# Output weights of a retention and bilinear kernel: six loads with casts on GpSimd, or six casting transfers from GpSimd's own DMA queue

## The chip, the core and the metric

The kernel runs on one core of one Trainium2 chip. The metric is device time in microseconds of one execution; before the change its median is 218.36 us over 3 runs (218.28 to 218.38).

## What is computed

A retention layer (linear attention with a decay for each head, 4 batches, 8 heads, 768 positions, head size 64) is followed by a bilinear feed-forward layer on 3072 tokens (model width 512, inner width 1536):

```python
for t in range(S):
    state = gamma * state + outer(k[:, :, t], v[:, :, t])      # per batch and head, 64 x 64
    y[:, :, t] = scale * q[:, :, t] @ state
x = y.transpose(0, 2, 1, 3).reshape(B * S, H * D)              # 3072 x 512
out = ((x @ w_a) * (x @ w_b)) @ w_out                          # w_a, w_b: 512 x 1536, w_out: 1536 x 512
```

All inputs and the output are f32. The change is about `w_out` alone.

## The kernel before

The 3072 positions are 24 chunks of 128. For each chunk GpSimd (or VectorE) multiplies k and q by a table of decays into a bf16 tile (`kqb`), a DMA transpose (later chunks) or TensorE (the first six) turns it into `kqT`, and TensorE forms masked scores (`at`, line 372), the running state (`st`, line 390) and the layer's output `y`. Finished chunks are gathered in groups of 4, 2, 2, 2, 2, 4 and 8 (`TILES`) for the feed-forward layer: `a` (line 568) and `g` (line 580) are the two products with `wa_bf` and `wb_bf`, ScalarE copies `a`, VectorE multiplies `g` with it into `ht`, and the product with `w_out` follows.

`w_out` lives on the chip as `wo_bf`, a bf16 tile of 128 partitions by 12 row blocks by 512 columns. It is used in three ways. For the first group, `ffn_out` (line 605) multiplies 4 pieces of 128 tokens with all 12 row blocks, 48 matmuls in the order of the blocks. For the later groups a Strassen-like scheme (`Group`, line 685) uses halves of `wo_bf` and sums of halves (`wsum`), which VectorE makes in `weight_sum` (line 618), right beside the first `ffn_out`. The first of these, `weight_sum(3)`, is two instructions on blocks 0 to 2 with 6 to 8, and 3 to 5 with 9 to 11.

Until the change `w_out` arrives in two steps. `load_o(j)`, called from the list `LOADS` through `issue_loads`, has SyncE's queue fetch two row blocks in f32 (512 KB, 2 KB to a packet) into a staging tile `wsto` of the pool `wstage` (6 buffers in turn, shared with the staging of the other weights and, later, with sums). `cast_o(j)` then has GpSimd cast it to bf16 into `wo_bf`. There are six of each (`NO`).

The order of the work on each engine is that of the program text: `seq` chains every instruction to the one before it on its engine. SyncE issues all loads of k, q, v and weights, the DMA transposes and the stores, one after the other, and a load that must wait for a buffer holds back all that is behind it. The entry of `LOADS` after the output weights, `s6`, loads chunks 6 and 7, and `t8` chunk 8; the DMA transposes of chunks 6 and 7 (line 333, in `casts_two`) come behind them. On GpSimd the six casts stand between the casts of v for the third pair of chunks (4 and 5) and the scaling of k and q for chunk 6 (line 292, from `casts_two(6)`).

Of the kernel before, what the change touches and what calls it, by code (L numbers as in the profile page):

```python
# [9 lines left out]
F32 = mybir.dt.float32  # L10
# [14 lines left out]
V_LATE = range(12, 20)  # L25
LACED = ("X3 X2 m1 m7 m2 a1 b1 a2 b2 m6 X1 a6 b6 a7 b7 F2 X4 m5 a5 b5 K20 G2 a3 b3 a4 b4 V18 "
         "m3 c1 d1 F3 H3 c2 d2 c6 d6 c7 d7 c5 d5 m4 c3 d3 V19 c4 d4 G3")
LOADS = "p0 p1 w0 w1 a1 b1 a2 k2 q2 b2 v2 o0 o1 o2 o3 o4 o5 s6 t8".split()


@with_exitstack
def kernel(
# [10 lines left out]
    nc = tc.nc  # L43
    P = 128
# [3 lines left out]
    DM = H * D  # L48
# [8 lines left out]
    FPO = NFT // NO  # L57
# [6 lines left out]
    wstage = ctx.enter_context(tc.tile_pool(name="wstage", bufs=6))  # L64
# [38 lines left out]
    def seq(bi):  # L103
        ins = bi.ins
        prev = last.get(ins.engine)
        if prev is not None:
            tc.add_manual_dep(ins, prev.name, nosync, reason="program order")
        last[ins.engine] = ins
        return bi
# [5 lines left out]
    raws, wst, whole = {}, {}, {}  # L115
# [19 lines left out]
    def load_two(nm, src, b, u, t):  # L135
        f = raw_tile([P, H, 2, D], F32, nm + "f", nm + "f")
        s = src[b, :, 2 * u * P : 2 * (u + 1) * P, :].rearrange("h (p two) d -> p h two d", two=2)
        seq(nc.sync.dma_start(out=f, in_=s))  # L138
        for par in range(2):
            raws[nm, t + par] = f[:, :, par, :]  # L140
# [5 lines left out]
    def load_wide(nm, n):  # L146
        src = {"a": moe_w_a, "b": moe_w_b}[nm]
        for i in range(2):
            st = wstage.tile([P, 2, 2 * WC], F32, tag="w", name="wst" + nm)
            s = src[2 * i * P : 2 * (i + 1) * P, 2 * n * WC : 2 * (n + 1) * WC]  # L150
            seq(nc.sync.dma_start(out=st, in_=s.rearrange("(c p) f -> p c f", p=P)))
            wst[nm, n, i] = st
# [7 lines left out]
            wst[nm, j] = st  # L160

    def load_o(j):
        st = wstage.tile([P, FPO, DM], F32, tag="w", name="wsto")
        s = moe_w_out[j * FPO * P : (j + 1) * FPO * P, :].rearrange("(c p) d -> p c d", p=P)
        seq(nc.sync.dma_start(out=st, in_=s))
        wst["o", j] = st

    pending = list(LOADS)

    def issue_loads(n):  # L170
        for _ in range(min(n, len(pending))):
            what = pending.pop(0)
            n = int(what[1:])
            if what[0] in "ab":
                load_wide(what[0], n)
            elif what[0] in "kqv":
                load_two(what[0], {"k": k, "q": q, "v": v}[what[0]], 0, n, 2 * n)
            else:
                {"p": load_pair, "s": load_slots, "t": load_slot, "w": load_w, "o": load_o}[what[0]](n)


    kqb = {}
    kqb = {}
    issue_loads(6)
    zero = osbp.tile([P, DM], F32, tag="osb", name="zero")
    seq(nc.vector.memset(zero, 0.0))
# [51 lines left out]
    wo_bf = wpool.tile([P, NFT, DM], BF16, name="wo_bf")  # L238
# [8 lines left out]
    def cast(engine, dst, src):  # L247
        if engine is nc.scalar:
            seq(nc.scalar.copy(dst, src))
        else:  # L250
            seq(engine.tensor_copy(dst, src))  # L251
# [8 lines left out]
    def cast_wide(nm, n):  # L260
        dst, c0 = {"a": wa_bf, "b": wb_bf}[nm], 2 * n * WC
        cast(nc.gpsimd, dst[:, :2, c0 : c0 + 2 * WC], wst[nm, n, 0])
        for i in range(2):
            c = slice(i * WC, (i + 1) * WC)
            cast(nc.gpsimd, dst[:, 2:, c0 + i * WC : c0 + (i + 1) * WC], wst[nm, n, 1][:, :, c])

    def cast_o(j):
        cast(nc.gpsimd, wo_bf[:, j * FPO : (j + 1) * FPO, :], wst["o", j])


    kb, qb, vb, kqT, aT = {}, {}, {}, {}, {}
# [808 lines left out]
    ffn_g(0, 0, 0, W2)  # L1080
    ffn_g(0, 1, 0, W2)
    issue_loads(100)
    cast_w(1, parts=2)
    ffn_a(0, 0, W2, 2 * W2)
# [30 lines left out]
    leave2(2, (A_, D_))  # L1115
    ffn_g(0, 11)
    for j in range(NO):
        cast_o(j)
    V_ = nc.vector

    def blocks(J, a, b):
# [147 lines left out]
```

## Time and profile before

| what | us |
| --- | --- |
| median of 3 runs | 218.36 |
| lowest and highest run | 218.28, 218.38 |
| span of the profiled execution | 216.6 |
| TensorE (PE) busy | 210.7 |
| GpSimd (POOL) busy | 154.2 |
| VectorE (DVE) busy | 147.5 |
| ScalarE (ACT) busy | 104.9 |
| one cast of a staging tile to `wo_bf`, of six | 1.04 |
| landing of one load of `wsto` after its issue, median | 8.7 |

The profile is one execution; its times count from the start of its span. The span leaves out what lies around the program on the device: 218.36 - 216.6 = 1.8 us beside the median of the runs. PE is TensorE's matmuls, PEld its weight loads, POOL is GpSimd, SPq the queue of DMAs that SyncE issues. A line of a timeline gives start, length, engine, line of the program, operation, what it writes and reads, how many, and in brackets how long the engine sat idle before and who ended that. "DMA to landing" counts from the issue to the arrival of the last byte.

### The profile page before, as it was taken

To read this page: it belongs to the slowest core of one execution; us is meant where nothing else is said; L and a number is where in the kernel's file an instruction comes from. 1 tells how busy PE (TensorE), PEld (TensorE's weight loads), DVE (VectorE), ACT (ScalarE), POOL (GpSimd) and SP (SyncE) were. 2 spreads that over 40 slices of the span, in tenths; PEclk is the share of its full clock that TensorE was granted. 3 is DMA by queue.
4 is the path that set the end of the run, shared out by engine and by line. 5 is a ranking of instruction groups with operands and counts; after the bars stand their busy time and mean duration, and the time that the engine had idled before them with its cause. 6 is when DMAs were issued, how large, how long until landed. Compare 5 with 4: busy or idle time off the path is not lost.

```text
span 216.6 us, 5713 instructions
## 1 busy us (share of the span) xinstructions
PE 210.7 (97%) x2252; PEld 146.1 (67%) x2252; DVE 147.5 (68%) x272; ACT 104.9 (48%) x235; POOL 154.2 (71%) x184
## 2 busy tenths in 40 slices
PE   7889999999999999999999999999999999999994
PEld 3557445587458888888888877457864444458883
DVE  3777346845984486356377978676577987688962
ACT  3256325343224444464576475657546656652331
POOL 5265876879878678969869979899986999530000
PEclk9999999999999999999999999999999999999999
DMA  5999999999999999999979999950013000000055
GB/s 162 290 320 365 387 311 360 384 268 232 221 264 227 228 231 222 158 192 269 197 169 245 222 209 234 236 127 3 5 69 125 2 0 3 2 0 0 27 194 170
DMA packets 85162, 39.68 MB, mean 183 GB/s; under 512 B 57488, under 2 KB 78864, under 8 KB 85136
## 3 DMA queue, kind: packets, MB, share of 16 engines
q1 hardware_dynamic: 84992, 39.26, 76.8%
q8 instruction: 17, 0.28, 0.5%
q14 instruction: 9, 0.07, 0.1%
q10 hardware_dynamic: 144, 0.07, 0.1%
HBM read 28.31 MB, written 6.29 MB: 160 GB/s over the span
## 4 chain that ended last, share of the span: by engine, by line
PE 91%; SPq 3%; DMA 3%; POOL 0%; issue 0%; DVE 0%
PE a L568 18%; PE g L580 18%; PE mA L685 12%; PE uA L859 10%; PE mB L685 6%; PE o L605 5%; PE uB L859 5%; SPq L138 3%; DMA wsta<-in_moe_w_a_dram 3%; PE mC L685 3%; PE at L372 2%; PE uC L859 2%; PE y L420 2%; PE st L390 2%; PE fa L949 2%; PE fb L949 1%
## 5 line engine op out<-in xcount | busy, mean ns | idle before, releaser
L582 DVE TENSOR_TENSOR ht<-g,asb 128x256 bf16<-128x256 f32 (+1 forms) x70 | 34.4, 493 | 31.6 <-PE g L580 28.0
L568 PE MATMUL a<-xt,wa_bf 128*128 128x256 bf16 (+1 forms) x280 | 48.6, 300 | 0.1
L580 PE MATMUL g<-xt,wb_bf 128*128 128x256 bf16 (+1 forms) x280 | 48.4, 300 | 0.0
L571 ACT CAST asb<-a 128x256 bf16<-128x256 f32 (+1 forms) x70 | 30.0, 429 | 33.3 <-PE a L568 31.1
L580 PEld LDWEIGHTS <-wb_bf 128*128 128x128 bf16 x280 | 27.0, 98 | 10.2 <-POOL wb_bf L251 0.2
L568 PEld LDWEIGHTS <-wa_bf 128*128 128x128 bf16 x280 | 26.5, 98 | 10.7 <-POOL wa_bf L251 0.4
L292 POOL TENSOR_TENSOR kqb<-kf,ktab 128x512 bf16<-128x512 f32 x22 | 23.6, 1078 | 7.4 <-DMA kf<-in_k_dram 4.9
L866 ACT COPY snap<-uA 128x512 f32<-128x512 f32 x36 | 20.0, 588 | 15.4 <-PE uA L859 13.9
L685 PEld LDWEIGHTS <-hs 128*128 128x128 bf16 x234 | 22.8, 98 | 3.6
L378 DVE TENSOR_TENSOR aT<-at,mask 128x512 bf16<-128x512 f32 x36 | 22.3, 682 | 0.3
L292 POOL TENSOR_TENSOR kqb<-qf,qtab 128x512 bf16<-128x512 f32 x18 | 19.6, 1088 | 2.7 <-DMA qf<-in_q_dram 2.7
L618 POOL TENSOR_TENSOR ht<-gsb,asb 128x512 bf16<-128x512 bf16 x13 | 15.2, 1175 | 7.5 <-DVE gsb L618 7.4
L692 ACT COPY snaps<-mA 128x256 f32<-128x256 f32 x30 | 11.0, 374 | 18.9 <-PE mA L685 18.9
L685 PEld LDWEIGHTS <-ht 128*128 128x128 bf16 x180 | 17.5, 98 | 3.3
L618 POOL TENSOR_TENSOR hs<-ht 128x384 bf16<-128x384 bf16 (+3 forms) x14 | 15.9, 1134 | 3.5 <-DVE ht L582 3.5
L618 POOL TENSOR_TENSOR hs<-ht,hs 128x384 bf16<-128x384 bf16 (+1 forms) x17 | 16.9, 997 | 1.5 <-DVE ht L582 1.4
L685 PE MATMUL mA<-wsum,hs 128*128 128x256 bf16 x120 | 15.2, 273 | 0.0
L618 DVE TENSOR_TENSOR osb<-mB,snaps 128x256 f32<-128x256 f32 x20 | 8.4, 421 | 8.3 <-ACT snaps L692 4.4
L251 POOL CAST vb<-vf 128x512 bf16<-128x512 f32 x12 | 7.5, 641 | 6.7 <-DMA vf<-in_v_dram 6.7
L605 PE MATMUL o<-wo_bf,ht 128*128 128x512 bf16 x48 | 10.7, 379 | 0.0
L618 DVE TENSOR_TENSOR asb<-uB,snap 128x512 bf16<-128x512 f32 x12 | 8.2, 685 | 3.1 <-ACT snap L866 2.0
L618 DVE TENSOR_TENSOR gsb<-uB,snap 128x512 bf16<-128x512 f32 x12 | 8.2, 686 | 2.9 <-ACT snap L866 2.1
(138 smaller groups left out, 374.7 us busy)
## 6 DMA issues: line engine op xcount, KB each, us to landing
qf<-in_q_dram SPq DMA_DIRECT2D x12, 512.0 KB, 6.1
out_dram<-osb SPq DMA_DIRECT2D x21, 256.0 KB, 4.1
kf<-in_k_dram SPq DMA_DIRECT2D x18, 256.0 KB, 5.1
vf<-in_v_dram SPq DMA_DIRECT2D x18, 256.0 KB, 5.3
wsta<-in_moe_w_a_dram SPq DMA_DIRECT2D x6, 512.0 KB, 7.7
wsto<-in_moe_w_out_dram SPq DMA_DIRECT2D x6, 512.0 KB, 8.7
wstb<-in_moe_w_b_dram SPq DMA_DIRECT2D x5, 512.0 KB, 8.3
kf<-in_k_dram SPq DMA_DIRECT2D x3, 512.0 KB, 7.1
```

The costliest lines, as they stand in the source:

```text
L292: seq(eng.tensor_tensor(dst, src, tab, op=ALU.mult))
L378: seq(nc.vector.tensor_tensor(aT[t][:, r], at[r], mask.to_broadcast([P, HP, P]), op=ALU.mult))
L568: seq(nc.tensor.matmul(a, wa_bf[:, kt, fs], xcols(J, kt, c0, c1), start=(kt == 0), stop=(kt == KT - 1)))
L571: seq(nc.scalar.copy(asb, a))
L580: seq(nc.tensor.matmul(g, wb_bf[:, kt, fs], xcols(J, kt, c0, c1), start=(kt == 0), stop=(kt == KT - 1)))
L582: seq(nc.vector.tensor_tensor(ht[J][:, ft, c0:c1], g, asbs.pop((J, ft, c0)), op=ALU.mult))
L605: seq(nc.tensor.matmul(o, ht[J][:, ft, i * P : (i + 1) * P], wo_bf[:, ft], start=(ft == 0), stop=(ft == NFT - 1), skip_group_check=True))
L618: seq(eng.tensor_tensor(dst, x, y, op=op))
L685: seq(nc.tensor.matmul(m, w, right[:, j], start=(first and j == 0), stop=(j == NP - 1), skip_group_check=True))
L692: seq(nc.scalar.copy(self.snaps[:, n], self.bank["A"]))
L859: seq(nc.tensor.matmul(m, w, right[:, k], start=(first and k == 0), stop=(k == 1), skip_group_check=True))
L866: seq(nc.scalar.copy(self.snaps[n], self.bank["A"]))
```

## The change

`load_o` no longer goes through SyncE and a staging tile. GpSimd issues the six transfers itself; each reads f32 from memory and writes bf16 into its part of `wo_bf`, so the cast happens in the transfer. The six casts are gone, and the six entries of `LOADS`. The transfers are issued where the casts stood in the program text.

```diff
-LOADS = "p0 p1 w0 w1 a1 b1 a2 k2 q2 b2 v2 o0 o1 o2 o3 o4 o5 s6 t8".split()
+LOADS = "p0 p1 w0 w1 a1 b1 a2 k2 q2 b2 v2 s6 t8".split()
...
     def load_o(j):
-        st = wstage.tile([P, FPO, DM], F32, tag="w", name="wsto")
         s = moe_w_out[j * FPO * P : (j + 1) * FPO * P, :].rearrange("(c p) d -> p c d", p=P)
-        seq(nc.sync.dma_start(out=st, in_=s))
-        wst["o", j] = st
+        seq(nc.gpsimd.dma_start(out=wo_bf[:, j * FPO : (j + 1) * FPO, :], in_=s))
...
-
-    def cast_o(j):
-        cast(nc.gpsimd, wo_bf[:, j * FPO : (j + 1) * FPO, :], wst["o", j])
...
     for j in range(NO):
-        cast_o(j)
+        load_o(j)
```

On GpSimd, between the casts of v for chunks 4 and 5 and the scaling of k and q for chunks 6 and 7, there stood before:

```order
L251 CAST vb<-vf 128x512 [waits DMAHW5_49]
L251 CAST vb<-vf 128x512
L251 CAST wo_bf<-wsto 128x1024 [waits DMAHW6_49]
L251 CAST wo_bf<-wsto 128x1024 [waits DMAHW7_49]
L251 CAST wo_bf<-wsto 128x1024 [waits DMAHW0_49]
L251 CAST wo_bf<-wsto 128x1024 [waits DMAHW1_49]
L251 CAST wo_bf<-wsto 128x1024 [waits DMAHW2_49]
L251 CAST wo_bf<-wsto 128x1024 [waits DMAHW3_49]
L292 TENSOR_TENSOR kqb<-kf,ktab_175 128x2x4x64 [waits DVE_49,DMAHW4_49,PE_49,Activation_49]
```

and with the change (line numbers of the changed file, 2 to 5 lower) there stands:

```order
L249 CAST vb<-vf 128x512 [waits DMAHW5_49]
L249 CAST vb<-vf 128x512
L164 DMA wo_bf<-in_moe_w_out_dram 128x2x512 x6
L287 TENSOR_TENSOR kqb<-kf,ktab_175 128x2x4x64 [waits DVE_49,DMAHW6_49,PE_49,Activation_49]
L287 TENSOR_TENSOR kqb<-qf,qtab 128x2x4x64 [waits DMAHW7_49]
```

Six casts that each waited for a load of SyncE became six DMA issues that wait for nothing of their own.

On SyncE, from the last load of the third pair of chunks on, there stood before:

```order
L138 DMA vf<-in_v_dram 128x8x128 [waits DMAHW5_49]
L165 DMA wsto<-in_moe_w_out_dram 128x2x512 [waits DMAHW6_49,Pool_49]
L165 DMA wsto<-in_moe_w_out_dram 128x2x512 [waits DMAHW7_49,Pool_49]
L165 DMA wsto<-in_moe_w_out_dram 128x2x512 [waits DMAHW0_49,Pool_49]
L165 DMA wsto<-in_moe_w_out_dram 128x2x512 [waits DMAHW1_49,Pool_49]
L165 DMA wsto<-in_moe_w_out_dram 128x2x512 [waits DMAHW3_49,DMAHW2_49,Pool_49]
L165 DMA wsto<-in_moe_w_out_dram 128x2x512 [waits DMAHW4_49,Pool_49]
L129 DMA kf<-in_k_dram 128x8x64
L138 DMA qf<-in_q_dram 128x8x128 [waits DMAHW5_49,DVE_49]
```

and with the change:

```order
L138 DMA vf<-in_v_dram 128x8x128 [waits DMAHW5_49]
L129 DMA kf<-in_k_dram 128x8x64 [waits DMAHW6_49]
L138 DMA qf<-in_q_dram 128x8x128 [waits DMAHW7_49,DVE_49]
L129 DMA kf<-in_k_dram 128x8x64 [waits DMAHW0_49]
L129 DMA vf<-in_v_dram 128x8x64 [waits DMAHW1_49]
```

The loads of chunks 6 to 8 moved up by six places.

On TensorE the order is the same; what the first product with `wo_bf` waits for is not. `o` is its result. Before:

```order
L605 LDWEIGHTS ht [waits DVE_49]
L605 MATMUL o<-wo_bf,ht 128x512 [waits Pool_49]
L605 LDWEIGHTS ht
L605 MATMUL o<-wo_bf,ht 128x512
L605 LDWEIGHTS ht
L605 MATMUL o<-wo_bf,ht 128x512 [waits Pool_49]
```

With the change:

```order
L600 LDWEIGHTS ht [waits DMASW0_49]
L600 MATMUL o<-wo_bf,ht 128x512 [waits DVE_49]
L600 LDWEIGHTS ht
L600 MATMUL o<-wo_bf,ht 128x512
L600 LDWEIGHTS ht
L600 MATMUL o<-wo_bf,ht 128x512 [waits DMASW1_49]
```

Each of the six waits for a cast by GpSimd is now a wait for one of GpSimd's transfers (DMASW0 to DMASW5), at every second matmul as before. VectorE's first `weight_sum` now waits for four of these transfers, and its second instruction for the other two.

More of the change, by code (lines that the diff above doesn't have):

```diff
@@ L178, in issue_loads @@
             else:
-                {"p": load_pair, "s": load_slots, "t": load_slot, "w": load_w, "o": load_o}[what[0]](n)
+                {"p": load_pair, "s": load_slots, "t": load_slot, "w": load_w}[what[0]](n)
     kqb = {}
```

## Prediction

> **What bounds the kernel now.** I read the page of the profile first (engine shares, the strip of 40 slices, the chain that ended last), then TensorE's waits, then a table by stretches around the place where the output weights are loaded and first used.
>
> ```profile
> span 216.6 us, 5713 instructions
> ...
> PE 210.7 (97%) x2252; PEld 146.1 (67%) x2252; DVE 147.5 (68%) x272; ACT 104.9 (48%) x235; POOL 154.2 (71%) x184
> ...
> DMA  5999999999999999999979999950013000000055
> ...
> PE 91%; SPq 3%; DMA 3%; POOL 0%; issue 0%; DVE 0%
> ```
>
> TensorE is busy 97% of the span and 91% of the chain of waits is TensorE. GpSimd (POOL) has 0% of the chain although it is 71% busy. The DMA engines are full for the first two thirds. So the question is whether TensorE ever waits for GpSimd or for a load.
>
> ```profile
> PE idle L552 <- DVE zero L186: 1.5, 1, 1.5
> PE tp L477 <- DVE kqb L292: 0.7, 3, 0.2
> PE idle L552 <- ACT kqT L249: 0.4, 1, 0.4
> ```
>
> That is the whole list of TensorE's waits: 2.6 us, none for a GpSimd cast and none for `wo_bf`. All three lines belong to the start of the program (warm-up matmuls and the first transposes); the rest of its idle time is the wait of the end for the last stores. The stretches around the change agree:
>
> ```profile
> 28.00:36.00 8.00, 8.00 (x51) 4.03 (x49) 4.85 (x7) 3.42 (x6) 5.44 (x8) 1.00 1.14 325
> 36.00:44.00 8.00, 8.00 (x123) 4.84 (x122) 6.34 (x11) 2.59 (x6) 6.34 (x8) 1.00 1.06 378
> 44.00:52.00 8.00, 8.00 (x75) 7.16 (x74) 3.82 (x9) 3.42 (x10) 6.13 (x7) 1.00 1.09 238
> 52.00:60.00 8.00, 8.00 (x43) 3.92 (x41) 7.50 (x10) 1.55 (x3) 6.81 (x8) 1.00 1.10 237
> ```
>
> The columns are start and end, length, then busy time and instructions of PE, PEld, DVE, ACT and POOL, the granted clock, the DMA share and GB/s. TensorE has 8.00 of 8.00 us in each stretch at a granted clock of 1.00: there is no idle time here that a faster GpSimd could return. The change can gain almost nothing; it can only lose, if TensorE begins to wait. The whole prediction is about deadlines.
>
> **The deadlines.** First use on TensorE, then on VectorE, then GpSimd's part as it stands:
>
> ```profile
> 52.66 7.93 PE L605 MATMUL o<-wo_bf,ht 128*128 128x512 bf16 x36
> 60.52 0.32 PE L390 MATMUL st<-vb,kqb 128*64 128x64 bf16 x8
> 60.76 0.64 PE L372 MATMUL at<-kqT 64*64 64x128 bf16 x32
> ```
>
> ```profile
> 53.27 1.86 DVE L618 TENSOR_TENSOR wsum<-wo_bf 128x768 bf16<-128x768 bf16 x2
> ```
>
> ```profile
> 37.70 1.18 POOL L251 CAST vb<-vf 128x512 bf16<-128x512 f32 x2 [0.59 <-DMA vf<-in_v_dram]
> 39.06 1.04 POOL L251 CAST wo_bf<-wsto 128x1024 bf16<-128x1024 f32 x1 [0.18 <-DMA wsto<-in_moe_w_out_dram]
> ...
> 45.87 1.04 POOL L251 CAST wo_bf<-wsto 128x1024 bf16<-128x1024 f32 x1 [0.38 <-DMA wsto<-in_moe_w_out_dram]
> 47.15 1.04 POOL L292 TENSOR_TENSOR kqb<-kf,ktab 128x512 bf16<-128x512 f32 x1 [0.23 <-PE a L568]
> ```
>
> The 36 matmuls of line 605 take 60.52 - 52.66 = 7.86 us, 0.22 us each. A sixth of `wo_bf` holds two of the twelve row blocks, so counting from 0, sixth j is wanted at 52.66 + 0.44 j: the first at 52.66 us, the last at 54.8 us. VectorE's first difference of weights (53.27) reads sixths 0, 1, 3 and 4, so it wants the fifth about a microsecond earlier than TensorE does; it can delay TensorE only later, through the work behind it. In before the last cast ends at 45.87 + 1.04 = 46.9 us: 5.7 us of slack before the first use.
>
> **Part by part: what leaves.** Six casts of 1.04 us (6.25 us) and the waits ahead of them (0.18 to 0.38 us each, 1.8 us in all) leave GpSimd: it went from 38.88 us (37.70 + 1.18) to 47.15 us with this block. Worth to TensorE: nothing, by the stretches above. Six issues leave SyncE's queue:
>
> ```profile
> 30.08 0.46 SPq L138 DMA_DIRECT2D vf<-in_v_dram  x1
> 30.63 6.88 SPq L165 DMA_DIRECT2D wsto<-in_moe_w_out_dram  x6
> 37.56 0.47 SPq L129 DMA_DIRECT2D kf<-in_k_dram  x1
> ...
> 51.83 4.17 SPq L333 DMA_TRANSPOSE kqT<-kqb  x2
> ```
>
> So the loads of k, q and v for chunks 6, 7 and 8, which began at 37.56, can begin at 30.63. That is earlier than needed and gains nothing either.
>
> **What comes.** Six DMA instructions on GpSimd at 38.88 us. They hold no wait, but they are behind everything GpSimd does until then: the transfers that were issued from 30.63 on now start over 8 us later. What one costs GpSimd no row shows. The nearest rows are the same transfer issued by SyncE and the cast that it replaces:
>
> ```profile
> L165 SPq DMA_DIRECT2D wsto<-in_moe_w_out_dram x6: 368/493/2011, 30.6 to 37.1; - x6
> ...
> DMA to landing us min/median/max: 8.1/8.7/9.6
> ```
>
> ```profile
> 38.12 3.90 SPq L138 DMA_DIRECT2D qf<-in_q_dram  x1
> ```
>
> The bounds are 0.37 us (SyncE's shortest for this transfer) and 3.9 us (its longest of any in this stretch, with the engines full). I take 1.04 us, the cast: GpSimd is then free at 38.88 + 6.24 = 45.1 us, 2 us earlier than before. Break-even against 47.15 is 1.38 us each. Behind the six stand the casts of chunks 6 and 7 and, on SyncE, the two transposes that wait for them:
>
> ```profile
> L333 SPq DMA_TRANSPOSE kqT<-kqb x2: 1250/2032/2813, 51.8 to 54.7; - x2
> ...
> DMA to landing us min/median/max: 3.2/4.1/5.0
> ```
>
> The second transpose lands at 54.7 + 3.2 = 57.9 us and TensorE reads it at 60.76, so GpSimd may be 2.9 us late: up to (47.15 + 2.9 - 38.88) / 6 = 1.86 us an issue before TensorE waits.
>
> The Trainium skill, "DMA: Bandwidth & Descriptors", section "Anatomy of one DMA", fits a GpSimd transfer at 2.0 us plus its bytes over 436 GB/s. By it one of these would take, as an estimate, 3.2 us, and six in a row with no overlap would end near 58 us instead of my 52; the same section says that most of the fixed part is waiting for the last byte, and the trace has six SyncE transfers overlapping (each 8.1 to 9.6 us to landing, all issued within 6.88 us), so I keep overlap. No row here shows GpSimd's own fixed part.
>
> **When the six land.** Now transfer rates, from three stretches in which one kind of load dominates (2 KB packets of the output weights, 256 B packets of k and v, 512 B packets at the start):
>
> ```profile
> 37.00:43.00 6.00, 6.00 (x80) 3.40 (x79) 5.44 (x9) 1.61 (x4) 4.42 (x6) 1.00 1.05 384
> 48.50:51.50 3.00, 3.00 (x30) 2.68 (x28) 1.59 (x4) 1.12 (x3) 2.37 (x3) 1.00 1.01 212
> 4.00:12.00 8.00, 7.32 (x86) 4.12 (x88) 5.99 (x11) 2.05 (x5) 2.65 (x4) 1.00 1.22 293
> ```
>
> A sixth (524 KB of f32) is 1.37 us of the engines at 384 GB/s, six are 8.2 us. Chunks 6 to 8 are six loads of 262 KB at 212 GB/s (1.24 us) and two of 524 KB at 293 GB/s (1.79 us): 11.0 us. The bare time to landing is read from the smallest transfer of the page:
>
> ```profile
> out_dram<-osb SPq DMA_DIRECT2D x1, 64.0 KB, 1.8
> ```
>
> which is 1.8 us. The v load ahead of them landed at 37.70, so its packets were through near 35.9 and the engines then work on chunks 6 to 8. When the first new transfer appears (38.88 + 1.04 = 39.9 us), 11.0 - 4.0 = 7.0 us of these are left, and the new 8.2 us compete with them; behind them come the transposes. How two queues share an engine no row shows. If they take turns packet by packet, a 2 KB packet (2048 B at 384/16 = 24 GB/s an engine, 85 ns) meets a 256 B one (19 ns) or a 512 B one (28 ns), so the new queue gets 75 to 82%. The six are through at 39.9 + 8.2/0.79 = 50.3 and land by 52.1 us. The sixths before it land about 1.7 us apart, so the first is there near 43.5: each has over 2 us to its deadline. If they share time equally, the last is through at 39.9 + 16.4 = 56.3 and lands at 58.1, or at 56.9 if SyncE's queue runs dry at 53.9. I take turns by packet, because a packet is the piece in which the engines' work stands in the trace.
>
> The Trainium skill, the same page, section "Queues, rings and completion order", has each engine go round its queues and drain a packet of typically 9 to 17 descriptors before it switches. With 16 rows of each kind that is 1.37 against 0.31 us, 82% for the new queue, and the sum would be as above; if the turns were of equal bytes it would be the equal-time rival below. No run so far shows two loaded queues.
>
> Casting inside the transfer is the other unknown. Its bounds are 0.68 us a sixth (by the bf16 bytes written, half as many) and 2.73 us (half the rate); I take 1.37 us, the f32 bytes read, which is the row's own.
>
> **Sum:** gain 0, loss 0 while every landing is ahead of its use. The profiled execution has a span of 216.6 us and the runs shown a median of 218.36 (218.28 to 218.38), 1.8 us around the span; what is around it I leave unchanged. Forecast 218.4 us.
>
> **Rivals.**
> *Equal shares* (16%). The queues share the engines by time, not by packet. For it: SyncE's queue is loaded without a break (DMA share 1.04 to 1.1 in every stretch above). Against it: the packet sizes differ eightfold. The last sixth lands 2.1 to 3.3 us after 54.8, TensorE waits at line 605 that long, and all behind it is late: about 221 us. It decides as soon as the new queue gets under 8.2/(54.8 - 1.8 - 39.9) = 63% of the engines.
> *Slow issue* (14%). GpSimd needs well over 1.86 us for one. At 2.5 us it is free at 53.9, 6.7 us late; the transposes land at 64.6 instead of 57.9 and TensorE waits 3.9 us at line 372 (what it may have waited before, for the last sixth, is part of it): about 222.3 us. At 3.9 us it would be some 12 us. For it: nothing in the trace shows GpSimd making a transfer. Against: SyncE makes one in 0.37 us when unhindered.
> *Slow cast* (13%). At half the rate the six take 16.4 us, at 79% of the engines 20.8 us, through at 60.7, landing at 62.5: TensorE waits 7.7 us, 226 us. It decides from about 1.3 times the plain rate.
> *A cost around the program* (5%): a queue that was not used before may add to what lies around the span, by an amount no row shows; I allow half a microsecond.
> *A small gain* (8%). GpSimd 2 us ahead and SyncE's loads 7 us ahead could remove delays of a tenth of a microsecond among the short matmuls; over 0.44 us would be needed to see it, and TensorE's own list holds no wait after the start to remove.
>
> **How the numbers follow.** No visible change has 44%, the likeliest single case, so the forecast is 218.4 us. A measurement of this kernel can tell about 0.2%, 0.44 us, from no change. Slower holds 16 + 14 + 13 + 5 = 48%, faster 8%. Slower altogether is a little likelier than no change, but it is spread over 219 to 226 us. The range runs from 217.8 (most of the small gain) to 222.6, which takes in equal shares and a slow issue up to 2.5 us, and leaves out the slow cast and the tails, under 2 in 10.
>
> **What would show it.** Right: in the changed profile TensorE's list has no line for `o` or `wo_bf`, the six issues take GpSimd about 1 us each from 38.9, the matmuls of line 600 (605 before) start at 52.7 and the first `at` at 60.8. Wrong: a TensorE wait on the DMA of `wo_bf` (equal shares, slow cast; the packets' own time tells which), or GpSimd's `kqb` later than 50 us with TensorE waiting for `kqT` (slow issue).

## The result, and the profile after

The median is **218.77 us** (9 runs, 218.64 to 219.47) against 218.28 us (9 runs, 218.19 to 218.38) of the kernel before beside it: ratio 1.0025, 95% interval 1.0015 to 1.0034. That is 0.49 us more: small, but every run of it lies above every run of before. The profiled execution's span went from 216.572 to 217.056 us, 0.484 us, so what lies around the span did not change.

The page of the changed kernel, engine shares, the strip of the DMA engines, the new queue and the chain that ended last:

```profile
span 217.1 us, 5711 instructions
...
PE 210.3 (97%) x2252; PEld 145.9 (67%) x2252; DVE 148.7 (68%) x272; ACT 104.8 (48%) x235; POOL 151.6 (70%) x184
...
DMA  6999999999999999999989999970022000000055
...
q0 software_dynamic: 1632, 1.57, 4.5%
...
PE 91%; SPq 3%; DMA 3%; POOL 0%; issue 0%; DVE 0%
```

Nothing moved at this scale, except that a queue `q0` appears: GpSimd's, with 1.57 MB (the bf16 bytes that it writes). TensorE's waits, the whole list again:

```profile
PE idle L547 <- DVE zero L184: 1.5, 1, 1.5
PE tp L472 <- DVE kqb L287: 1.1, 3, 0.5
PE idle L547 <- ACT kqT L247: 0.4, 1, 0.4
```

No line for `o` and none for `wo_bf`. The first uses on TensorE stand where they stood:

```profile
52.71 7.93 PE L600 MATMUL o<-wo_bf,ht 128*128 128x512 bf16 x36
60.57 0.32 PE L385 MATMUL st<-vb,kqb 128*64 128x64 bf16 x8
60.82 0.64 PE L367 MATMUL at<-kqT 64*64 64x128 bf16 x32
```

Each is 0.05 us later than before, as is the last matmul of the program (it starts at 213.32 instead of 213.27). GpSimd's timeline around the change, and the six transfers as a group:

```profile
38.88 4.50 POOL L164 DMA_DIRECT2D wo_bf<-in_moe_w_out_dram  x6
43.36 1.10 POOL L287 TENSOR_TENSOR kqb<-kf,ktab 128x512 bf16<-128x512 f32 x1
...
51.10 0.61 POOL L249 CAST vb<-vf 128x512 bf16<-128x512 f32 x1 [3.12 <-DMA vf<-in_v_dram]
53.61 1.16 POOL L287 TENSOR_TENSOR kqb<-kf,ktab 128x512 bf16<-128x512 f32 x1 [1.90 <-DMA kf<-in_k_dram]
```

```profile
L164 POOL DMA_DIRECT2D wo_bf<-in_moe_w_out_dram x6: 732/750/900, 38.9 to 42.6; - x6
...
DMA to landing us min/median/max: 5.4/8.4/11.1
```

Six issues take 4.50 us. The transfers land at 44.28, 45.80, 48.15, 50.30, 51.55 and 53.68 us (the first is 38.88 + 5.4, the last 42.6 + 11.1). TensorE wants the last at 52.71 + 5 x 0.44 = 54.9, so it comes 1.2 us ahead. GpSimd is 3.8 us ahead of before at 43.36, and then waits 3.12 and 1.90 us for loads of chunks that TensorE reads only after 60 us.

**Where the half microsecond is.** SyncE's work ends with a walk: it checks the semaphores of all DMA queues (and two of VectorE and ScalarE, numbers 100 and 107 in the trace), two to an instruction, and then the program ends. These are the rows of that walk on the program's last line, of before and of after (number, duration in ns, first and last start):

```profile
L1264 SPq EVENT_SEMAPHORE  x7: 17/28/28, 214.8 to 216.5; - x7
```

```profile
L1259 SPq EVENT_SEMAPHORE  x10: 17/28/28, 215.7 to 217.0; - x10
```

Three more checks: GpSimd's six transfers brought six semaphores, which six of SyncE's eight are paired with. But the number alone is not it. After the last store has landed (215.65 before, 215.70 after), what is still to be walked differs. Of after, the stretch from 215.75 to 216.19, and of before all from 215.66 to the end:

```profile
L1259 SPq EVENT_SEMAPHORE  x7: 27/28/28, 215.8 to 216.2; - x7
```

```profile
L1264 SPq EVENT_SEMAPHORE  x4: 17/22/28, 215.7 to 216.5; - x4
L1264 SPq DRAIN  x3: 7/7/13, 215.8 to 216.1; - x3
```

After: the store's own pair is checked at 215.72, and these seven follow, 0.44 us at about 0.065 us each. Before: the first of the four is the store's own pair (215.67), one more follows (215.73), and the last two belong to the drains behind the walk, which both kernels have. From the landing of the last store to the end it is 0.92 us before and 1.35 us after: 0.43 of the 0.484 us. The rest is the 0.05 us that the last store is later.

Not all of the 0.43 us is the walk. From the check of the store's own pair to the first drain behind the walk it is 0.13 us before and 0.51 after, 0.38 more, for six more pairs. From that drain to the end it is 0.78 and 0.83 us. GpSimd clears semaphores there, and SyncE's last check waits for it; the clear takes longer after than before:

```profile
L1264 POOLq EVENT_SEMAPHORE_RANGE_CLEAR  x1: 96/96/96, 216.2 to 216.2; - x1
```

```profile
L1259 POOLq EVENT_SEMAPHORE_RANGE_CLEAR  x1: 139/139/139, 216.6 to 216.6; - x1
```

The place in the walk is set by which of SyncE's eight semaphores the last store gets: they go round, one for each DMA that SyncE issues (and one for the single store that ScalarE issues). The last store in the order of the two kernels, before and after:

```
118 L754 DMA out_dram<-osb 128x128 [waits DMAHW6_49,DVE_49]
112 L749 DMA out_dram<-osb 128x128 [waits DMAHW0_49,DVE_49]
```

Six issues fewer on SyncE shift it by six of eight, from the seventh semaphore (number 109 in the trace) to the first (101). The walk goes 105 and 104, 106 and 103, 108 and 101, 109 and 100, 110 and 107 before the change; afterwards 101 with GpSimd's 116 is the first pair of eight. Before, the walk is nearly over when the last store lands; now it waits at its first pair and has seven to go.

### The profile page after: what moved, and what is told of

Its sections match the earlier page's. It is cut to its first block, busy times and chain, and to the rows that moved or that the text cites. A ratio compares the mean times of both kernels' runs of the same rounds, so it can differ in the third digit from the quotient of the medians.

```text
span 217.1 us, 5711 instructions
## 1 busy us (share of the span) xinstructions
PE 210.3 (97%) x2252; PEld 145.9 (67%) x2252; DVE 148.7 (68%) x272; ACT 104.8 (48%) x235; POOL 151.6 (70%) x184
## 3 DMA queue, kind: packets, MB, share of 16 engines
q0 software_dynamic: 1632, 1.57, 4.5%
## 4 chain that ended last, share of the span: by engine, by line
PE 91%; SPq 3%; DMA 3%; POOL 0%; issue 0%; DVE 0%
PE a L563 18%; PE g L575 18%; PE mA L680 12%; PE uA L854 10%; PE mB L680 6%; PE o L600 5%; PE uB L854 5%; SPq L138 3%; DMA wsta<-in_moe_w_a_dram 3%; PE mC L680 3%; PE at L367 2%; PE uC L854 2%; PE y L415 2%; PE st L385 2%; PE fa L944 2%; PE fb L944 1%
```

## The experiments

The expectations letter the theories. **A**: the half microsecond is the walk at the end, and depends on which semaphore the last store has. The rivals **B** and **C** have it come with GpSimd's transfers as such (its queue in use and its semaphores to be checked; work that they hold up in the body), whatever semaphore the last store has. **D** came up later, for a scatter between runs: the last transfer lands too near its use.

**after_lane**: the changed kernel with seven loads of q cut in two, so that the last store gets the semaphore that is checked last (110). All of GpSimd's transfers stay.

```diff
-        seq(nc.sync.dma_start(out=f, in_=s))
+        if nm == "q" and t in (10, 12, 14, 16, 18, 20, 22):
+            for r in range(2):
+                hs4 = slice(HP * r, HP * (r + 1))
+                seq(nc.sync.dma_start(out=f[:, hs4], in_=s[:, hs4]))
+        else:
+            seq(nc.sync.dma_start(out=f, in_=s))
```

> The changed kernel with seven loads of q (chunks 10 to 22) cut into two halves of four heads each, so that SyncE issues seven DMAs more and the last store of the program uses another of the eight DMA semaphores, the one that SyncE checks last at the end of the program. Theory A (the loss is made at the end: after the last store has landed SyncE still checks seven pairs of semaphores, 0.065 us a pair, because six more semaphores stand in the list and the last store's is now checked first): no pair is left to check after the landing, about 0.45 us less than the change, 218.3 us, level with before within 0.1 us. Theory B (GpSimd's queue costs its 0.4 us at the end or around the span however the checks are ordered): 218.75 us as the change. Theory C (TensorE loses it on the way): 218.75 us, with the last matmul later than in before.

Measured: 218.29 us (11 runs, 218.18 to 218.35) beside 218.26 of before, ratio 0.9999 (0.999 to 1.0008). The rows of the walk until the last store lands at 215.68 us, and from there:

```profile
L1264 SPq EVENT_SEMAPHORE  x7: 27/28/28, 214.2 to 215.5; - x7
```

```profile
L1264 SPq EVENT_SEMAPHORE  x3: 17/17/28, 215.7 to 216.5; - x3
L1264 SPq DRAIN  x3: 7/7/13, 215.8 to 216.1; - x3
```

Seven pairs are done before the landing, the eighth holds the last store (the first of the three checks), none is left. The end is 0.92 us behind the landing, as in before. The loss is gone with all six transfers in place: C falls, and B as the main part. A small part of B stays: GpSimd's clear takes 0.139 us here too, and from the first drain to the end it is 0.84 us, 0.06 over before. The kernel is level with before because it has one pair less to go behind the store.

**before_lane**: the other way round, the kernel before with five loads of q cut in two by the same lines (chunks 14 to 22), so that the last store gets number 105, in the first of the five pairs. No transfer of GpSimd's is in it.

```diff
+        if nm == "q" and t in (14, 16, 18, 20, 22):
```

> The kernel before with five loads of q (chunks 14 to 22) cut into two halves, nothing else: the last store now uses a semaphore that SyncE checks first of its five pairs instead of fourth. Theory A: four pairs to check after the landing instead of one, 3 x 0.065 = 0.2 us more than before, 218.5 us, with no GpSimd transfer in the program. Theories B and C: 218.3 us, as before.

Measured: 218.52 us (11 runs, 218.40 to 218.58), ratio 1.0011 (1.0002 to 1.0019): 0.26 us over before. Four pairs are left when the store lands at 215.74, and the end is 1.11 us behind it. Of the 0.26 us, 0.19 are the walk (1.11 - 0.92), the rest a last store that is 0.07 us later.

**before_spare**: the kernel before with six casting transfers at the end of GpSimd's program, into `wa_bf`, which nothing reads any more. Nothing is left out of the computation.

```diff
     big()
+    spare = wa_bf.rearrange("p a (b c) -> p (a b) c", c=DM)
+    for j in range(NO):
+        s = moe_w_out[j * FPO * P : (j + 1) * FPO * P, :].rearrange("(c p) d -> p c d", p=P)
+        seq(nc.gpsimd.dma_start(out=spare[:, j * FPO : (j + 1) * FPO, :], in_=s))
```

> The kernel before with six casting transfers of the output weights by GpSimd added at the end of its program, where GpSimd and the DMA engines have nothing else to do; they write over the weights of the first product, which nothing reads any more, and nothing waits for them but the end of the program. Theory A: SyncE checks eight pairs instead of five, but the last store keeps a semaphore near the end of the list, so nothing is left to add: 218.3 us, as before. Theory B: 0.4 us more, 218.7 us. It also measures the transfer by itself: with an empty set of engines I expect 0.75 us an issue as in the changed kernel, and 1.4 us between landings if casting costs the engines nothing beyond the f32 read, 2.7 if it halves their rate.

Measured: 218.32 us (11 runs, 218.19 to 219.06), ratio 1.0006 (0.9997 to 1.0014). Eight pairs are walked, but the last store still has 109, one pair is left, and the end is 0.96 us behind its landing: the 0.04 us over before are again the longer clear (0.138 us). Together:

| kernel | pairs in the walk | last store's semaphore | pairs left at its landing | landing to end, us | median, us |
| --- | --- | --- | --- | --- | --- |
| before | 5 | 109 | 1 | 0.92 | 218.28 |
| before_spare | 8 | 109 | 1 | 0.96 | 218.32 |
| after_lane | 8 | 110 | 0 | 0.92 | 218.29 |
| before_lane | 5 | 105 | 4 | 1.11 | 218.52 |
| after | 8 | 101 | 7 | 1.35 | 218.77 |

The time goes with the fourth column, not with the second; that GpSimd's transfers are there adds about 0.05 us.

The same run shows the six transfers nearly alone, at a time when SyncE's queue has little to do. The DMA queues from 193 to 206 us:

```profile
q0 software_dynamic: 1627, 1.57, 81.7%
q1 hardware_dynamic: 140, 0.13, 3.8%
```

They are packets of 1 KB (the bf16 written), about 104 ns each (81.7% of 16 engines' 13 us over 1627). From the first packet (195.5 us) to the last (206.5) it is 11.0 us, 1.8 us a transfer. In the changed kernel, against a loaded SyncE queue, it is 12.0 us (40.9 to 52.9): the load from SyncE slowed GpSimd's queue by about a tenth. The landings from the first to the last lie 53.68 - 44.28 = 9.4 us apart there; here 206.97 - 197.85 = 9.1 us.

**spare_plain**: is it the cast that makes a transfer take 1.8 us? The same six, f32 into f32, over `wa_bf` and `wb_bf` seen as f32 (nothing reads them any more; nothing is left out).

```diff
-    spare = wa_bf.rearrange("p a (b c) -> p (a b) c", c=DM)
     for j in range(NO):
+        spare = (wa_bf, wb_bf)[j // 3].rearrange("p a f -> p (a f)").bitcast(F32)
+        spare = spare[:, j % 3 * FPO * DM : (j % 3 + 1) * FPO * DM]
```

> The kernel before with six transfers by GpSimd of the same f32 data at the end of its program, as in before_spare, but without the cast: f32 into the place of the two other weights, which nothing reads any more. Nothing uses them. It separates the cast from the queue. In before_spare the six took 10.9 us alone (1.8 us each, 96 to 98 ns a packet). If casting is what costs, the six take about 8.2 to 8.6 us here, 1.4 us each, and 85 to 88 ns a packet as on SyncE's queue. If GpSimd's queue is what costs, they stay near 10.9 us. Time 218.3 us either way.

Measured: 218.22 us (one run). From 193 to 206 us:

```profile
q0 software_dynamic: 862, 3.14, 67.8%
q1 hardware_dynamic: 141, 0.13, 2.9%
```

Packets of 4 KB now and half as many, but 10.8 us for the six. The engines are 14 points less busy and the transfers hardly faster, so neither the cast nor full engines set this pace. It was seen only on GpSimd's queue: SyncE's six in the kernel before landed 1.36 us apart on average (39.01 to 45.82). What sets the pace was not found.

The Trainium skill, "DMA: Bandwidth & Descriptors", section "Bandwidth", gives 6.15 us and 341 GB/s for a transfer of 1 MB issued from GpSimd. The two do not go together if each byte is counted once: 1 MB in 6.15 us is some 170 GB/s, as an estimate from that row. Here 3.15 MB in six overlapping transfers take 10.8 us, 291 GB/s counted once, faster than the row's time would have it and slower than its rate; no run here has a single transfer of 1 MB, and the measurement decides for transfers of this size.

**late_issue**: how much slack is there, and what does a late transfer cost? The changed kernel with the six issues behind `casts_two(6)`, so 6.1 us later (44.97).

```diff
-    for j in range(NO):
-        load_o(j)
...
     casts_two(6)
+    for j in range(NO):
+        load_o(j)
```

> The changed kernel with the six transfers issued after GpSimd's casts of chunks 6 and 7 instead of before them, about 9 us later. In the changed kernel the last of the six landed at 53.7 us, about 1.1 us before TensorE wants it. By the deadlines of the prediction, the last should land at 58 to 63 us and TensorE wait 4 to 8 us at the first product with the output weights, all of it in the time: 222.5 to 227 us. If the first product could start late without loss (other work of TensorE in its place), the time would stay under 219.5.

Measured: 226.01 us (one run). TensorE's waits have a first line now, and TensorE's timeline shows each wait:

```profile
PE o L600 <- DMA wo_bf<-in_moe_w_out_dram: 4.3, 5, 1.2
```

```profile
52.69 0.59 PE L600 MATMUL o<-wo_bf,ht 128*128 128x512 bf16 x2
54.08 0.59 PE L600 MATMUL o<-wo_bf,ht 128*128 128x512 bf16 x2 [0.79 <-DMA wo_bf<-in_moe_w_out_dram]
55.73 0.59 PE L600 MATMUL o<-wo_bf,ht 128*128 128x512 bf16 x2 [1.06 <-DMA wo_bf<-in_moe_w_out_dram]
57.51 1.01 PE L600 MATMUL o<-wo_bf,ht 128*128 128x512 bf16 x2 [1.18 <-DMA wo_bf<-in_moe_w_out_dram]
```

The sixths land at 52.16, 54.04, 55.69, 57.47, 59.06 and 60.71 us. TensorE waits 4.3 us, yet the last matmul is 7.3 us later. The stretches say why (columns as before; the granted clock is third from the end):

```profile
52.00:60.00 8.00, 4.38 (x18) 1.70 (x17) 1.41 (x3) 0.37 (x1) 1.38 (x3) 0.80 1.22 196
60.00:64.00 4.00, 3.36 (x10) 1.21 (x9) 3.20 (x5) 0.59 (x1) 1.36 (x2) 0.55 1.12 225
```

A mean of 0.80 over 8 us and of 0.55 over 4 us is a clock of 0.5 for 1.6 / 0.5 + 1.8 / 0.5 = 6.8 us, from 56.75 us on, during the third wait: the same two matmuls take 1.01 instead of 0.59 us. The waits cost about 1.7 times their own length.

The Trainium skill, "TensorE: Matmul & The Clock Gate", Part 1, has the clock halved after an idle window of 3.4 us and restored after a busy one. The half rate and the length (two such windows) agree with this trace; the condition does not read the same here, since no wait was over 1.2 us and TensorE worked between them, 1.2 us of the 3.4 us ahead of the drop.

**early_issue**: is there a better place, ahead of everything in this block? The six issues ahead of the scaling of k for chunks 4 and 5, at 30.78 us.

```diff
     cast_wide("a", 2)
+    for j in range(NO):
+        load_o(j)
     casts2(2, {(K, 0): G_, (K, 1): G_}, ("b", 2))
...
-    for j in range(NO):
-        load_o(j)
     V_ = nc.vector
```

> The changed kernel with the six transfers issued 8 us earlier, ahead of GpSimd's scaling of k for chunks 4 and 5, near 31 us instead of 38.9. If the new queue takes turns with SyncE's by packet (2 KB against 512 B: three quarters or more of the engines), the loads that are due then, the last part of the second weight and v of chunks 4 and 5, land 5 to 8 us later than now and TensorE waits for them, 4 to 8 us, and loses more than it waits if the clock drops: 223 to 230 us. If the queues shared equally by time, those loads would be about 4 us late and the loss 2 to 4 us. If the new queue had to wait its turn behind SyncE's backlog, no loss beyond the 2 us that GpSimd's issues take ahead of the scaling.

Measured: 223.88 us (one run). The landings are early (37.55 to 47.42 us), but TensorE waits for GpSimd itself:

```profile
PE tp L472 <- POOL kqb L287: 3.1, 2, 2.5
```

```profile
30.78 4.50 POOL L164 DMA_DIRECT2D wo_bf<-in_moe_w_out_dram  x6
35.26 2.13 POOL L287 TENSOR_TENSOR kqb<-kf,ktab 128x512 bf16<-128x512 f32 x2
```

The 4.5 us of issuing hold back the scaling that the first transposes wait for. The time lies in the expected range by another way than the expected one: v of chunks 4 and 5 did land 4.8 us later than in the changed kernel (42.53 against 37.71), but no wait of TensorE is on it. The last matmul is 5.1 us later (218.41) for 3.1 us of waiting: again the granted clock goes to 0.5, here for 3.4 us from 37.3.

**two_transfers**: two transfers of half the matrix instead of six; is an issue's price one of size?

```diff
+        n = NFT // 2
...
-    for j in range(NO):
+    for j in range(2):
         load_o(j)
```

> The changed kernel with the six casting transfers joined into two of three sixths each, at the same place. Only two semaphores of GpSimd's queue are left instead of six. Theory A: the end checks six pairs instead of eight, the last store's semaphore is in the second pair and four pairs come after it, where the change has seven and before one: 3 x 0.065 = 0.2 us over before, 218.45 us, and 0.25 us under the change, if the second transfer still lands by 54 us, where TensorE and VectorE want it. Theory B (a fixed cost of GpSimd's queue): 218.75 us. For the issue: 0.75 us each as now if an issue has a fixed price, about 2.2 us each if it goes by packets (768 instead of 256).

Measured: 219.06 us (12 runs, 218.46 to 219.96), ratio 1.0036 (1.0023 to 1.0048). An issue of three times the size takes hardly longer:

```profile
L165 POOL DMA_DIRECT2D wo_bf<-in_moe_w_out_dram x2: 837/928/1020, 38.9 to 39.9; - x2
...
DMA to landing us min/median/max: 9.0/11.3/13.5
```

The lowest run is where A puts it (six pairs, four left, 218.45), but the runs scatter over 1.5 us. The second half lands at 53.43 us in this profile and is wanted with the seventh of twelve row blocks, at 52.71 + 6 x 0.22 = 54.0: theory D.

**two_slack** tried to bring that landing forward by moving the load of chunk 8 on SyncE's queue behind the transposes.

```diff
-LOADS = "p0 p1 w0 w1 a1 b1 a2 k2 q2 b2 v2 s6 t8".split()
+LOADS = "p0 p1 w0 w1 a1 b1 a2 k2 q2 b2 v2 s6".split()
...
+        load_slot(t + 2)
         load_slot(t + 3)
```

> two_transfers with the loads of chunk 8 taken out of SyncE's backlog and issued behind the transposes of chunks 6 and 7, so that less competes with the two casting transfers and the second lands earlier. two_transfers ran at 218.46 in its best run, as theory A had it (218.45), but scattered up to 219.96; in its profile the second transfer landed at 53.43 us, where VectorE wants it at 53.3 and TensorE at 54.0. Theory D (the scatter is the second transfer landing up to 1.5 us too late in some runs): with it landing a microsecond earlier the scatter goes and the median is 218.45 to 218.5. Theory E (the scatter is something else, for instance the start of the program): it stays, with a median near 219.

Measured: 219.41 us (6 runs, 218.58 to 220.09), ratio 1.0058 (1.0046 to 1.007). Its premise failed: with loads moved off SyncE's queue the second half still lands at 53.41, which fits the small difference to the spare transfers. It does not test D.

**two_again**: two_transfers unchanged, for another profile.

> two_transfers again, for a second profile. Theory D: if the run is over 218.8 us, TensorE's waits show the first product waiting for wo_bf by about the excess, and the second transfer landed after 54 us; if it is at 218.5, no such wait. Theory E: an excess with no wait at that product.

Measured: 219.84 us (one run), at the upper end of that scatter:

```profile
PE o L601 <- DMA wo_bf<-in_moe_w_out_dram: 0.6, 1, 0.6
...
PE mA L681 <- POOL hs L614: 0.4, 1, 0.4
```

The second half landed at 54.59 us, 1.2 us later than in the first profile and 0.6 us too late; the last matmul is 1.3 us later than in after. D holds for this execution.

**two_sooner**: the same two transfers issued 5.5 us earlier (33.38), inside `casts2`, where GpSimd waits for weights anyway.

```diff
         if between is not None:
+            for j in range(2):
+                load_o(j)
             cast_wide(*between)
...
-    for j in range(2):
-        load_o(j)
     V_ = nc.vector
```

> two_transfers with both issued about 5 us earlier, near 33.6 us, where GpSimd otherwise waits 1 us for the last part of the second weight. two_slack did not test theory D: its second transfer landed at 53.4 us as before, since it does not go faster when SyncE loads less. Two_again bore theory D out (second landing 54.59 us, 0.6 us of TensorE waiting at the first product, and VectorE's sums 1.4 us late). Here the second should land at 48 to 50 us, 4 us ahead of its use. Theory D: the scatter goes, all runs within 0.4 us, median 218.45 to 218.6 (four pairs checked after the last store). Theory E: scatter and median as in two_transfers, near 219. What could spoil it: the loads of the second weight and of v for chunks 4 and 5, which the new transfers now meet, landing late enough for TensorE to wait; then the median is higher, with a wait in TensorE's list near 39 us and no scatter at the first product.

Measured: 218.59 us (11 of 12 runs within 218.44 to 218.83, one of 220.78; of before one of 17 is at 220.28), ratio 1.0015 (0.9993 to 1.0037). The halves land at 43.56 and 48.91 us and the scatter is gone but for that one run, which stays unexplained. What is left over before, some 0.3 us, is where A puts four pairs (before_lane: 0.26).

No version is faster than the kernel before; after_lane is level with it.

## Why the prediction came out as it did

The 218.77 us lie 0.37 over the forecast of 218.4 and inside its range. The forecast rested on deadlines, and these held. The sum was "gain 0, loss 0 while every landing is ahead of its use", and TensorE's list shows just that. What the sum lacked is a term for the end of the program: it put the loss at 0 for any landings in time, and the end became 0.43 us longer all the same. "What is around it I leave unchanged" held, since all but 0.01 us lies inside the span. The nearest rival was "a cost around the program", 5% and half a microsecond. The size was that, but not the place or the reason: it lies inside the span, behind the last landing, and comes from the shift of SyncE's semaphores, with the number of pairs as its multiplier; a cost of the new queue as such is the 0.05 us of the longer clear. How large the miss came out is an accident of the count: seven pairs to go is the most that eight can leave, and with seven more DMAs on SyncE after_lane has none. Nothing in TensorE's waits could show it. The trace of before did hold it: the walk of five pairs stood in its last 2 us, and the six issues that leave SyncE were counted without asking what they shift.

- *Issue on GpSimd.* I took 1.04 us; it is 0.75 (0.73 to 0.90). GpSimd was free at 43.4 instead of 45.1. The rival of the slow issue (1.86 us and more) falls. early_issue shows what such time costs where it is not covered.
- *Casts and SyncE's issues that leave.* Worth nothing, as said: GpSimd's gain went into waits of 3.12 and 1.90 us for loads.
- *When the six land.* I forecast 43.5 for the first and 52.1 for the last; measured 44.28 and 53.68. The mechanism for sharing held in its result: the new queue kept most of its pace, and the equal shares that would have put the last at 56.9 or later fall. The mis-sized term is the transfer itself: 1.37 us by SyncE's rate, 1.8 us even alone. My 79% for the share was too low (11.0 us alone against 12.0 is 92%), and the two errors partly cancel: that the last landing is only 1.6 us off is in part luck. The first packet came at 40.9 us where I had 39.9, and the first transfer needs longer to land beside SyncE's loads (5.4 us after its issue, 3.9 in before_spare, 4.6 in my forecast). The margin is 1.2 us where I had 2.7.
- *Slow cast.* A transfer takes 1.3 times what I assumed, right at the point from which that rival would decide, and the reason is not the cast: spare_plain has the same pace. It did not decide, because the queue kept more of its pace than the 79% in that sum.
- *A small gain.* None seen.
- *The break-even.* late_issue moved the issues by 6.1 us and lost 7.3 us at the last matmul. The rivals' times were worked out as if TensorE lost only what it waits; with the halved clock they would have been worse.
- *A reading.* The DMA shares of the four stretches around the change are 1.06 to 1.14, where "equal shares" has 1.04 to 1.1; no number hangs on it.

The changed kernel's own runs reach from 218.64 to 219.47, more than before's. A last sixth that lands late in some runs would do that, as in two_again, but no profile of such a run of it was taken, and after_lane, with the same six transfers (the last lands at 53.33 us), has 11 runs within 0.17 us. So this stays open.

## What to carry over

Count what a change does to the end of the program: which semaphore the last store gets and how many are checked behind it; a few issues more or fewer on the storing queue are worth up to 0.4 us here. A transfer moved to GpSimd's queue costs GpSimd 0.7 to 1.0 us for its issue, whether it moves 512 KB or 1.5 MB, so issue few, where GpSimd waits anyway. Leave such a transfer more than a microsecond to its deadline, since the second landing moved by 1.2 us between two executions of two_transfers, and waits of 3 to 4 us on TensorE cost about 1.7 times their length here.

## What the runs showed of the hardware

- SyncE's checks at the end take about 0.065 us a pair and go in one order up to the first that has to wait; those behind the last store's own pair cost time (0 to 7 pairs: 0.92 to 1.35 us from landing to end). GpSimd's clear behind them takes 0.096 us in the kernels without its transfers and 0.138 to 0.142 in those with them.
- GpSimd's queue moves six transfers of 512 KB in 11.0 us (cast) or 10.8 (plain) alone, in packets of 1 KB (written) or 4 KB, where SyncE's 2 KB packets went at 384 GB/s in the kernel before. Beside a loaded SyncE queue it took 12.0 us, and SyncE's loads landed later, up to 13.3 us after their issue. From 40 to 54 us of after, both queues at once:

```profile
q0 software_dynamic: 1632, 1.57, 69.7%
q1 hardware_dynamic: 4814, 1.46, 50.5%
...
vf<-in_v_dram SPq DMA_DIRECT2D x2, 256.0 KB, 10.6
qf<-in_q_dram SPq DMA_DIRECT2D x1, 512.0 KB, 13.3
kf<-in_k_dram SPq DMA_DIRECT2D x1, 256.0 KB, 12.7
```

- The shares add up to over 100%: packets of the two queues overlap on an engine. The longest landing of a `qf` was 10.6 us before.
- With five waits of TensorE of 0.6 to 1.2 us the granted clock went to 0.5 for 6.8 us, from the third wait on (late_issue); with waits of 2.5 and 0.6 us, to 0.5 for 3.4 us (early_issue). With two waits of 0.6 and 0.4 us it stayed at 1.00 (two_again).
